# Attention tiles of 32 rows: scores from 64x32 weight tiles, value products from 32x64 weight tiles, one turn per head pair

## The chip, the cores and the metric

The kernel is one program on one core of a Trainium2 chip. The metric is the device time of that program in microseconds (us). Its engines are named as in the profile: PE is the matrix engine (PEld its weight loads), DVE the vector engine, ACT the scalar engine, POOL the GpSimd engine, SP the queue that issues the DMAs.

## The reference

Eight batches of eight heads, 576 positions, head size 64. The first four heads look back 32 positions, the last four look back 128 positions in steps of 4. Then comes a mixing block on the 512 joined channels.

```python
mask_plain = (rel >= 0) & (rel < window)                       # window = 32
mask_dil = (rel >= 0) & (rel < window * dilation) & (rel % dilation == 0)   # dilation = 4
scores = np.where(masks, scale * np.matmul(q, k.transpose(0, 1, 3, 2)), -1e9)
attn = softmax(scores)
x = np.matmul(attn, v)          # joined over the heads: (8, 576, 512)
theta = x @ w_theta
y = einsum('ts,bsd->btd', w_tok_r, x * cos(theta)) + einsum('ts,bsd->btd', w_tok_i, x * sin(theta))
u = x + y
return u + np.maximum(u @ w_ch, 0.0)
```

All arithmetic is to float32 accuracy. The host only puts q, k and v in other orders; heads with steps of 4 are put in the order position mod 4, position div 4, so that every head looks back 32 rows.

## The kernel before, in words

**Work.** A batch b has four head pairs pr (two heads hh = 0, 1 in each). The 576 query rows of a head are cut into 18 blocks of QB = 32 rows. Block qb needs the 64 key columns from 32 before its start to its end (BW = 64). Two blocks (e = 0, 1) of both heads make one group of 128 rows, so that a pair has NJ = 9 groups j.

**Scores** (`scores`, L585). The host writes q with zeros: for each block a 128x64 weight tile, whose rows are the two heads' 64 channels, and whose columns are head 0's 32 queries (rows of head 1 zero) and head 1's (rows of head 0 zero). A product of that tile with 64 key columns (L614) gives 64 rows of scores, two for a group, 18 a pair, in two PSUM banks (groups 0 to 4, 5 to 8). DVE adds the mask and takes the row maximum (L553), ACT takes the exponential (L649), DVE the sum and its reciprocal (L652, L653), POOL multiplies (L655). The result is P, 128 rows by 9 x 64.

**Turn** (`turn`, L659). The value product needs P with keys on the partitions. DVE turns P in eight transposes of 32 rows by 288 (L673), for hh, e and o (o is the first or second 32 of the 64 keys), into pt, a tile with zeros set once by POOL, where group j and head hh have a 128x64 block: rows of e = 0 against columns of e = 0, rows of e = 1 against columns of e = 1, zeros between. For batch 0 `flip` (L691) does it on PE (L709), with copies by DVE (L684) and ACT (L687).

**Value products** (`pv`, L757). For a group and a head, 128 rows of v (the two blocks' 64 keys) by 64 channels are the weights, and pt's 128x64 block moves (L773): 18 products a pair, into one PSUM tile "o" of 576 columns. ACT copies it to x (L733), for the last two pairs in the natural order of positions.

**The rest.** theta (L842), sine and cosine, and the token mixing in split form, high and low parts of about half the bits each. From batch 2 on the token mixing is done in fourteen "steps" (L1235, `fast_step`, PSUM tiles A to D) instead of L1444; then channel mixing (L1477).

**What sets the order.** A recorder (`Order`) keeps tasks with ranks and planned costs and writes the instructions of all engines in the order in which its plan starts them. In the first part (batch 0, batch 1 up to its token mixing) ranks decide (`RANK`). From batch 1's token mixing on (`steady`, `phase`) PE's order is a written list: scores of the next batch's pairs are put before steps by `S_FAST`, value products behind steps by `PV_FAST`, so that three of a batch's four score blocks stand right behind a value product. Costs in `yield "PE", ...` and in `phase` only move the plan.

**Loads.** SP loads q (576 KB a pair), k (304 KB), v in two parts (320 and 256 KB), two pairs ahead.

Of the kernel before, what the change touches and what calls it, by code (L numbers as in the profile page):

```python
# [18 lines left out]
DM = H * D  # L19
# [4 lines left out]
VA = 5  # L24
NC = DM // 128
# [187 lines left out]
SLACK = 500  # L213
LATENCY = dict(PE=100.0, DVE=100.0, ACT=130.0, POOL=130.0, DMA=1800.0)
# [35 lines left out]
def build(ctx, tc, qT, kT, vw, wth, wtk, wch, maskb, ident, identb, outT):  # L250
# [60 lines left out]
    def load_qk(n):  # L311
        if n >= B * NP:
            return
        b, pr = divmod(n, NP)
        yield "rank", due.get(("scores", b, pr), od.rank)
        r = yield from take("qk", 2)
        if od.steady and b > FIRST and pr < 2:
            yield None, ("vbi", b - 1, pr + 1)
        q = ap.tile([128, 2 * NJ, 2 * QB], F32, tag="q", name=f"q{b}_{pr}")
        k = ap.tile([128, S + 32], F32, tag="k", name=f"k{b}_{pr}")  # L320
        yield "DMA", dma(2 * S)
        pin(nc.sync.dma_start(q, qT[b, pr]))
        yield "DMA", dma(S + 32)
        pin(nc.sync.dma_start(k, kT[b, pr]))
        qks[b, pr] = (q, k, r)
        signal(("qk", b, pr))
# [51 lines left out]
    KE = S + 32  # L378
# [11 lines left out]
    mskb = cp.tile([128, 6, BW], BF16, name="mskb")  # L390
# [5 lines left out]
    def first_loads():  # L396
# [3 lines left out]
        for pr in range(NP):  # L400
# [4 lines left out]
            q = q.rearrange("p a b -> p (a b)").rearrange("p (a b) -> p a b", b=2 * QB)  # L405
            k = first_k[:, KE * pr:KE * pr + KE]
            yield "DMA", dma(2 * S)
# [19 lines left out]
    def consts():  # L427
# [4 lines left out]
        for n in range(2):  # L432
            t = cp.tile([128, NJ, 2, 2 * QB], F32, name=f"pt{n}")
            yield "POOL", 1040
            pin(nc.gpsimd.memset(t, 0.0))
            pts.append(t)
# [99 lines left out]
    def mask_of(pr, j):  # L536
        if j == 0:
            return 1
        return {2: 2, 4: 3, 6: 4, 7: 5}.get(j, 0) if pr >= NP // 2 else 0

    pmats, probs = {}, {}

    def strips():

        for hh in range(2):
            for e in range(2):
                for o in range(2):
                    yield hh, e, o
# [9 lines left out]

    def on_pe(b, pr):
        return b == 0  # L560
# [24 lines left out]
    def scores(b, pr):  # L585
        yield None, ("qk", b, pr)
        if b == 1 and on_pe(b, pr):
            yield None, "sin0"
# [11 lines left out]
        for g0, g1 in ((0, 5), (5, NJ)):  # L600
            ps, rel = yield from bank("s", f"s{b}_{pr}_{g0}")
            ps = ps[:, :(g1 - g0) * BW].rearrange("p (a b) -> p a b", b=BW)
            held[g0] = ps, rel
            if b == 2 and not od.steady:
                yield "LATER", SLACK
            masked = on_pe(b, pr)
            if masked:
                yield "PE", 150
                mask_on_pe(ps, pr, g0, g1)
            yield "PE", (148 if od.steady else 162) * (g1 - g0)  # L610
            for n in range(g0, g1):
                for e in range(2):
                    qb = 2 * n + e
                    pe(nc.tensor.matmul(ps[64 * e:64 * e + 64, n - g0], q[:, qb],  # L614
                                        k[:, QB * qb:QB * qb + BW], start=not masked, stop=not masked or n == g1 - 1))
            if masked:
                go(row_max(b, ps, rel, P, mx, g0, g1, ("mask", b, pr, g0)))
            else:
                go(mask_scores(ps, rel, P, mx, pr, g0, g1, ("mask", b, pr, g0)))
# [7 lines left out]
        if b and on_pe(b, pr):  # L627
            for g0, (ps, rel) in held.items():
                yield None, ("mask", b, pr, g0)
                yield "EXP", 335 * ps.shape[1]  # L630
                for n in range(ps.shape[1]):
                    table(nc.scalar.activation(P[:, g0 + n], ps[:, n], AF.Exp, bias=mx[:, g0 + n:g0 + n + 1],
                                               scale=SCALE, accum_out=sm[:, g0 + n, :1]))
                give(*rel)
        else:
            for g0 in (0, 5):
                yield None, ("mask", b, pr, g0)
# [5 lines left out]
        elif not on_pe(b, pr):  # L643
# [15 lines left out]
    def turn(b, pr):  # L659
# [4 lines left out]
        yield None, ("pv",) + divmod(b * NP + pr - 2, NP)  # L664
        P, rp = probs.pop((b, pr))
        pmats[b, pr] = pts[pr % 2]
        for i, (hh, e, o) in enumerate(strips()):
            if od.steady:
                yield "TURN" if i < 7 else "DVE", 482
            elif i % 2 == 0:  # L670
                yield "DVE", 940
            k0, p0 = QB * (2 * e + o), QB * (2 * e + hh)
            pin(nc.vector.transpose(pmats[b, pr][k0:k0 + QB, :, hh, QB * e:QB * e + QB],  # L673
                                    P[p0:p0 + QB, :, QB * o:QB * o + QB]))
        give("P", rp)
        signal(("pt", b, pr))

    def flip_evac(b, ps, rel, pr, g0, g1, key):
        for e in range(2):
            es, qs = slice(BW * e, BW * e + BW), slice(QB * e, QB * e + QB)  # L680
            n = (g1 - g0) * BW
            if e == 0:
                yield "DVE", dve(n)
                pin(nc.vector.tensor_copy(pmats[b, pr][es, g0:g1, :, qs], ps[es]))  # L684
            else:
                yield "ACT", act(n)
                pin(nc.scalar.copy(pmats[b, pr][es, g0:g1, :, qs], ps[es]))  # L687
        give(*rel)
        signal(key)

    def flip(b, pr):  # L691

        yield None, ("P", b, pr)
        if pr >= 1:
            yield None, ("fl", b, pr - 1)
        if b or pr >= 2:
            yield None, ("pv",) + divmod(b * NP + pr - 2, NP)
        yield None, "pts"
        pmats[b, pr] = pts[pr % 2]
        P, rp = probs.pop((b, pr))  # L700
        gs = (0, 5), (5, NJ)
        for i, (g0, g1) in enumerate(gs):
            ps, rel = yield from bank(FL0[i] if b == 0 else "xt"[i], f"pT{b}_{pr}_{g0}")
            ps = ps[:, :(g1 - g0) * BW].rearrange("p (a h b) -> p a h b", h=2, b=QB)
            yield "PE", 70 * (g1 - g0)
            for n in range(g0, g1):
                for e in range(2):
                    es = slice(BW * e, BW * e + BW)
                    pe(nc.tensor.matmul(ps[es, n - g0].rearrange("p a b -> p (a b)"), P[es, n], idt[es, es],  # L709
                                        start=True, stop=True))  # L710
            go(flip_evac(b, ps, rel, pr, g0, g1, ("fe", b, pr, g0)))
        signal(("fl", b, pr))
        for g0, _ in gs:
            yield None, ("fe", b, pr, g0)
        if b == 0:
            give(f"xh{pr}", 0)
        else:
            give("P", rp)
# [4 lines left out]
    def x_evac(b, pr, ps, rel, key):  # L723
        dst, src = xf[b, pr], ps
        if pr >= NP // 2:
            dst = dst.rearrange("p (j c) -> p c j", c=4)
            src = src.rearrange("p (c j) -> p c j", c=4)
# [29 lines left out]
    def pv(b, pr):  # L757
# [10 lines left out]
        ps = ps_v.tile([128, 2 * DM], F32, tag="v", name=f"o{b}_{pr}")[:, :S]  # L768
        yield "PE", 1060 if od.steady else 1300
        for j in range(NJ):  # L770
            v = va[:, j] if j < VA else vb[:, j - VA]
            for hh in range(2):
                pe(nc.tensor.matmul(ps[64 * hh:64 * hh + 64, BW * j:BW * j + BW], v[:, 64 * hh:64 * hh + 64],  # L773
# [963 lines left out]
```

## Time and profile before

| | |
|---|---|
| three runs, us | 555.21, 554.04, 555.28 (median 555.21) |
| profiled execution, us | 555.45 |
| its span, first to last instruction, us | 553.7 |
| granted PE clock, mean | 0.994 |
| busy, us: PE, PEld, DVE, ACT, POOL | 528.7, 478.8, 435.5, 373.1, 329.4 |
| instructions on PE and PEld | 5296 each |
| data moved by DMA | 124.42 MB, mean 225 GB/s |

The span is the time between the first and the last instruction; 1.75 us of the profiled execution lie outside it. A float32 product appears as two records on PE and two on PEld: the 18 score products of a pair are 36 records. A matmul record is long (222 ns for 64 columns), since it holds the way through the array; what counts is the distance from one record's start to the next. In rows of instructions "128*64 128x64" means a weight tile of 128 rows by 64 columns, and an output or operand of 128x64.

### The profile page before, as it was taken

Reading aid. Unit: us, or ns where it says so; the run is one execution under the profiler, and the core shown is the slowest. Engines: PE = TensorE matmul, PEld = TensorE weight load, DVE = VectorE, ACT = ScalarE, POOL = GpSimd, SP = SyncE. Lnnn points to the kernel's source line nnn. Section 1 sums busy time; section 2 is a strip of 40 time slices with the busy share of each in tenths; the row PEclk is TensorE's granted clock in tenths of the full one; section 3 lists DMA queues with packets and bytes.
Section 4 is the critical chain, followed back from the end, with each engine's and each line's share of the span. In section 5 each row is a group of like instructions: output and inputs, shape, how many; then the busy total and the mean of one; then the engine's idle time right before and its main releaser. Section 6 shows DMA issues by size and latency. Waiting matters only on the chain.

```text
span 553.7 us, 14354 instructions
## 1 busy us (share of the span) xinstructions
PE 528.7 (95%) x5296; PEld 478.8 (86%) x5296; DVE 435.5 (79%) x1359; ACT 373.1 (67%) x1029; POOL 329.4 (59%) x347
## 2 busy tenths in 40 slices
PE   5798898999999999999999999999999999999997
PEld 4643887888899899989999899989999899989997
DVE  3878897995588797989799988989799978848322
ACT  1589977858928478768775786768776777467320
POOL 1327868899774175655468375646468365817660
PEclk9999799999999999999999999999999999999999
DMA  8985245633578938994599828993698727680722
GB/s 297 400 332 186 99 139 202 222 144 119 165 256 265 343 155 283 341 282 173 189 326 306 299 86 274 363 281 118 236 325 282 277 90 219 209 274 28 233 85 86
DMA packets 59127, 124.42 MB, mean 225 GB/s; under 512 B 5424, under 2 KB 24624, under 8 KB 58800
## 3 DMA queue, kind: packets, MB, share of 16 engines
q1 hardware_dynamic: 59056, 123.49, 65.1%
q8 instruction: 42, 0.69, 0.5%
q14 instruction: 29, 0.24, 0.1%
HBM read 99.88 MB, written 23.59 MB: 223 GB/s over the span
## 4 chain that ended last, share of the span: by engine, by line
PE 65%; DVE 10%; DMA 9%; ACT 7%; POOL 5%; issue 2%; SPq 1%; POOLq 0%; ACTq 0%; DVEq 0%
PE c L1477 15%; PE th L842 11%; PE C L1235 8%; PE A L1235 7%; PE D L1235 6%; PE o L773 5%; PE B L1235 4%; PE s L614 4%; DVE pt L673 4%; DMA va<-in_vw_dram 3%; PE y L1444 2%; PE th L824 2%; DMA xn<-xd 1%; DMA st_wtk<-in_wtk_dram 1%; DMA q<-in_qT_dram 1%
## 5 line engine op out<-in xcount | busy, mean ns | idle before, releaser
L673 DVE STREAM_TRANSPOSE pt<-P 32x288 f32<-32x288 f32 x224 | 105.1, 469 | 13.1 <-POOL P L655 8.8
L1477 PE MATMUL c<-u,late_wc 128*128 128x288 f32 x768 | 109.1, 296 | 1.2 <-DVE x L1453 1.0
L1477 PEld LDWEIGHTS c<-u,late_wc 128*128 128x128 f32 x768 | 105.5, 188 | 4.7 <-DVE x L1453 1.5
L649 ACT ACTIVATE P<-P,mx 128x64 f32<-128x64 f32 x252 | 84.4, 337 | 2.9 <-DVE mx L553 2.6
L842 PE MATMUL th<-wthh,xh 128*128 128x512 f32 x224 | 75.0, 395 | 0.2 <-DVE K L1377 0.2
L655 POOL TENSOR_TENSOR P<-P,mx 128x576 f32<-128x576 f32 x32 | 38.2, 1192 | 57.6 <-DVE mx L653 50.4
L553 DVE CUSTOM_DVE_ANT_0 P<-s,mskb 128x64 f32<-128x64 f32 x252 | 39.0, 218 | 18.0 <-PE s L614 17.7
L1251 ACT CAST u<-x 128x288 fp32r<-128x288 f32 x48 | 20.6, 430 | 45.3 <-DVE x L1261 44.8
L842 PEld LDWEIGHTS th<-wthh,xh 128*128 128x128 f32 x224 | 42.0, 188 | 9.6 <-DVE K L1377 0.4
L1253 POOL TENSOR_TENSOR u<-x,u 128x288 fp32r<-128x288 f32 x48 | 41.6, 872 | 14.4 <-ACT u L1251 14.0
L649 ACT ACTIVATION_READ_ACCUMULATOR P<-P,mx 128x1 f32 x252 | 47.3, 188 | 0.0
L842 PE MATMUL th<-wthl,xh 128*128 128x512 f32 x112 | 44.4, 396 | 0.0
L733 ACT COPY x<-o 128x576 f32<-128x576 f32 x32 | 29.4, 920 | 19.6 <-PE o L773 19.5
L489 POOL TENSOR_TENSOR zl<-g,zh 128x512 fp32r<-128x512 f32 x7 | 9.1, 1298 | 53.5 <-ACT zh L481 53.5
L614 PE MATMUL s<-k,q 128*64 128x64 f32 x1008 | 36.6, 225 | 2.7 <-DVE K L1377 2.2
L614 PEld LDWEIGHTS s<-k,q 128*64 128x64 f32 x1008 | 32.8, 139 | 7.1 <-issue 2.7
L1453 DVE SCALAR_TENSOR_TENSOR x<-c,x 128x288 f32<-128x288 f32 x64 | 28.4, 451 | 11.6 <-PE c L1477 11.4
L773 PEld LDWEIGHTS o<-pt,va 128*64 128x64 f32 x600 | 20.4, 137 | 11.7 <-DVE pt L673 3.2
L773 PE MATMUL o<-pt,va 128*64 128x64 f32 x600 | 24.8, 227 | 5.8 <-DVE pt L673 2.9
L1015 POOL TENSOR_TENSOR s<-f,x 128x256 f32<-128x256 f32 x24 | 17.8, 740 | 12.2 <-DVE f L1003 10.0
L842 PEld LDWEIGHTS th<-wthl,xh 128*128 128x128 f32 x112 | 21.0, 188 | 4.2
L1095 POOL TENSOR_TENSOR s1l<-s,s1h 128x512 fp32r<-128x512 f32 x12 | 15.4, 1288 | 14.0 <-ACT s1h L1092 14.0
(232 smaller groups left out, 1576.3 us busy)
## 6 DMA issues: line engine op xcount, KB each, us to landing
q<-in_qT_dram SPq DMA_DIRECT2D x32, 576.0 KB, 6.0
late_wt_a<-tw_t SPq DMA_DIRECT2D x24, 576.0 KB, 6.8
wt_g<-tw_b SPq DMA_DIRECT2D x22, 576.0 KB, 6.4
va<-in_vw_dram SPq DMA_DIRECT2D x30, 320.0 KB, 4.9
k<-in_kT_dram SPq DMA_DIRECT2D x28, 304.0 KB, 6.2
out_dram<-x SPq DMA_DIRECT2D x28, 288.0 KB, 2.1
vb<-in_vw_dram SPq DMA_DIRECT2D x29, 256.0 KB, 4.5
xd<-xq SPq DMA_DIRECT2D x24, 288.0 KB, 5.3
```

What stands on the lines that cost most here:

```text
L553: pin(nc.vector.tensor_tensor_reduce(out=P[:, n], in0=ps[:, n - g0], in1=mskb[:, mask_of(pr, n)], op0=ALU.add, op1=ALU.min, scale=-SCALE, ...
L614: pe(nc.tensor.matmul(ps[64 * e:64 * e + 64, n - g0], q[:, qb], k[:, QB * qb:QB * qb + BW], start=not masked, stop=not masked or n == g1 - 1))
L649: table(nc.scalar.activation(P[:, n], P[:, n], AF.Exp, bias=mx[:, n:n + 1], scale=-1.0, accum_out=sm[:, n, :1]))
L655: pin(nc.gpsimd.tensor_tensor(P, P, mx.unsqueeze(2).to_broadcast([128, NJ, BW]), op=ALU.mult))
L673: pin(nc.vector.transpose(pmats[b, pr][k0:k0 + QB, :, hh, QB * e:QB * e + QB], P[p0:p0 + QB, :, QB * o:QB * o + QB]))
L733: pin(nc.scalar.copy(dst, src))
L773: pe(nc.tensor.matmul(ps[64 * hh:64 * hh + 64, BW * j:BW * j + BW], v[:, 64 * hh:64 * hh + 64], pmats[b, pr][:, j, hh], start=True, stop=T ...
L842: pe(nc.tensor.matmul(pt, l, r, start=(n == 0), stop=(n == 3 * NC - 1)))
L1235: pe(nc.tensor.matmul(ps, l, r, start=first and n == 1, stop=last and n == 3 * len(ks), skip_group_check=more))
L1253: pin(nc.gpsimd.tensor_tensor(ul[b, d][:, ts], x[:, ts], uh[b, d][:, ts].bitcast(F32), op=ALU.subtract))
L1453: pin(nc.vector.scalar_tensor_tensor(out=x[:, ts], in0=ps, scalar=0.0, in1=x[:, ts], op0=ALU.max, op1=ALU.add))
L1477: pe(nc.tensor.matmul(ps, l[:, cs], r[:, ts], start=(n == 0), stop=(n == 3 * NC - 1)))
```

## The change

Queries are stored without zeros. A head's 576 rows are cut in two halves of 9 blocks: e is now the half, and group n has block n of both halves of both heads (qb = n + 9 e). A score product has a weight tile of 64 rows (one head's channels) by 32 queries. A pair has 36 of them instead of 18, each with 64 key columns, written to one 32-row strip of a bank. For batches from 1 on the two banks are both taken first, and the products go in turn to the first bank and the second. The host swaps the two heads in the second bank's groups, so that the eight products for one group of each bank have eight different places in the array: two halves of its rows by four quarters of its columns.

The turn is one transpose of 128 rows by 576 (each 32x32 block in place), in batch 0 too; `flip`, its copies, the zeroed pt tiles and their POOL memsets are gone. A value product has 32 rows of v (one head, one half e, keys o) by 64 channels as its weights, and 32 columns of pt move. A pair has 72 of them instead of 18; the two products o = 0, 1 of a group accumulate in the same place, so that four places of the array are used (four quarters of its rows; e and the head pick them, the head picks the half of its columns). The halves e go to two PSUM banks.

q is 288 KB a pair instead of 576, k 352 instead of 304, v the same size in another order. The plan's costs are other numbers.

```diff
-        q = ap.tile([128, 2 * NJ, 2 * QB], F32, tag="q", name=f"q{b}_{pr}")
-        k = ap.tile([128, S + 32], F32, tag="k", name=f"k{b}_{pr}")
+        q = ap.tile([128, 2 * NJ, QB], F32, tag="q", name=f"q{b}_{pr}")
+        k = ap.tile([128, KE], F32, tag="k", name=f"k{b}_{pr}")
...
-                    pe(nc.tensor.matmul(ps[64 * e:64 * e + 64, n - g0], q[:, qb],
-                                        k[:, QB * qb:QB * qb + BW], start=not masked, stop=not masked or n == g1 - 1))
+        def block(n, e):
+            qb = n + NJ * e
+            ko = QB * (qb + 1 + 2 * e + (n >= JS)) - QB
+            for r in range(2):
+                rs, to = slice(64 * r, 64 * r + 64), QB * (2 * e + (r if n < JS else 1 - r))
+                ps = held[0 if n < JS else JS][0]
+                pe(nc.tensor.matmul(ps[to:to + QB, n % JS], q[rs, qb], k[rs, ko:ko + BW],
+                                    start=b > 0, stop=b > 0 or n in (JS - 1, NJ - 1)))
...
+            yield "PE", SC_NS
+            for i in range(JS):
+                for g0, g1 in groups:
+                    if g0 + i < g1:
+                        for e in range(2):
+                            block(g0 + i, e)
...
-            pin(nc.vector.transpose(pmats[b, pr][k0:k0 + QB, :, hh, QB * e:QB * e + QB],
-                                    P[p0:p0 + QB, :, QB * o:QB * o + QB]))
+        pin(nc.vector.transpose(pmats[b, pr], P.rearrange("p n (o s) -> p (n o) s", s=QB)))
...
-            for hh in range(2):
-                pe(nc.tensor.matmul(ps[64 * hh:64 * hh + 64, BW * j:BW * j + BW], v[:, 64 * hh:64 * hh + 64],
-                                    pmats[b, pr][:, j, hh], start=True, stop=True))
+            for o in range(2):
+                for e in range(2):
+                    for hh in range(2):
+                        rs = slice(QB * (2 * e + hh), QB * (2 * e + hh) + QB)
+                        pe(nc.tensor.matmul(ps[64 * hh:64 * hh + 64, e, QB * j:QB * j + QB], v[rs, 64 * o:64 * o + 64],
+                                            pmats[b, pr][rs, 2 * j + o], start=(o == 0), stop=(o == 1)))
...
-        go(flip(0, p), RANK["flip"][p])
+        go(turn(0, p), RANK["flip"][p])
```

PE's list at one place of the steady part, before: between step products into D and C stand the value products of the third pair (o_3) and the scores of the next batch's pair 1 (s_1_0 and s_1_5 are its two banks). "x10" is ten equal products in a row.

```order
L1235 MATMUL D_1_4941<-late_wt_b,s1l_4799 128x288
L773 MATMUL o_3_4972<-pt_118,va_3_4756 64x64 x10
L773 MATMUL o_3_4972<-pt_118,vb_3_4836 64x64 x8
L614 MATMUL s_1_0_4997<-k_1_4759,q_1_4758 64x64 x10
L614 MATMUL s_1_5_5018<-k_1_4759,q_1_4758 64x64 x8
L1235 MATMUL C_0_4865<-late_wt_a,i2h_4889 128x288 x2
```

The same place of the changed kernel:

```order
L1184 MATMUL D_1_5232<-late_wt_b,s1l_5030 128x288
L724 MATMUL o_3_5262<-pt_117,va_3_4980 64x32 x40
L724 MATMUL o_3_5262<-pt_117,vb_3_5112 64x32 x32
L595 MATMUL s_1_0_5341<-k_1_4983,q_1_4982 32x64 x4
L595 MATMUL s_1_5_5342<-k_1_4983,q_1_4982 32x64 x4
L595 MATMUL s_1_0_5341<-k_1_4983,q_1_4982 32x64 x4
L595 MATMUL s_1_5_5342<-k_1_4983,q_1_4982 32x64 x4
L595 MATMUL s_1_0_5341<-k_1_4983,q_1_4982 32x64 x4
L595 MATMUL s_1_5_5342<-k_1_4983,q_1_4982 32x64 x4
```

The blocks keep their places among the steps; 18 and 18 products have become 72 and 36, and the scores alternate between the banks.

DVE's list in the last batch before, where pair 2's and pair 3's turns (L673) stand among additions of step results (L1261, L1273):

```order
L673 STREAM_TRANSPOSE pt_116<-P_2_6357 32x9x32
L1261 TENSOR_TENSOR x_0_5508<-B_0_6462,x_0_5508 128x288
L673 STREAM_TRANSPOSE pt_116<-P_2_6357 32x9x32
L1261 TENSOR_TENSOR x_1_5639<-B_1_6480,x_1_5639 128x288
L652 TENSOR_REDUCE mx_3_6434<-sums_97 128x9
L653 RECIPROCAL mx_3_6434<-mx_3_6434 128x9
L673 STREAM_TRANSPOSE pt_116<-P_2_6357 32x9x32 x6
L1273 TENSOR_TENSOR x_2_5713<-A_0_6381,x_2_5713 128x288
L673 STREAM_TRANSPOSE pt_118<-P_3_6433 32x9x32
```

The same place now (the turn is L662, xq is the turn of x for the batch after):

```order
L1210 TENSOR_TENSOR x_0_7031<-B_0_8316,x_0_7031 128x288
L662 STREAM_TRANSPOSE pt_116<-P_2_8125 128x576
L1210 TENSOR_TENSOR x_1_7234<-B_1_8330,x_1_7234 128x288
L645 TENSOR_REDUCE mx_3_8274<-sums_97 128x9
L646 RECIPROCAL mx_3_8274<-mx_3_8274 128x9
L846 STREAM_TRANSPOSE xq_8318<-x_1_8395 128x18x32
L1222 TENSOR_TENSOR x_2_7356<-A_0_8165,x_2_7356 128x288
L662 STREAM_TRANSPOSE pt_117<-P_3_8273 128x576
```

Each pair's eight transposes have become one, and the additions stand closer together.

More of the change, by code (lines that the diff above doesn't have):

```diff
@@ L432, in consts @@
         for n in range(2):
[L433 to L436, printed above, removed]
+            pts.append(cp.tile([128, 2 * NJ, QB], F32, name=f"pt{n}"))
         signal("pts")
@@ L536, in mask_of @@
     def mask_of(pr, j):
-        if j == 0:
-            return 1
-        return {2: 2, 4: 3, 6: 4, 7: 5}.get(j, 0) if pr >= NP // 2 else 0
+        if pr < NP // 2:
+            return int(j == 0)
+        return {0: 2, 4: 3, 5: 4}.get(j, 0)
     pmats, probs = {}, {}
-    def strips():
-        for hh in range(2):
-            for e in range(2):
-                for o in range(2):
-                    yield hh, e, o
     def mask_scores(ps, rel, P, mx, pr, g0, g1, key):
@@ L603, in scores @@
             held[g0] = ps, rel
+            if b == 0:
+                yield "PE", 150
+                mask_on_pe(ps, pr, g0, g1)
+                yield "PE", 125 * (g1 - g0)
+                for n in range(g0, g1):
+                    for e in range(2):
+                        block(n, e)
+                go(row_max(b, ps, rel, P, mx, g0, g1, ("mask", b, pr, g0)))
+        if b:
             if b == 2 and not od.steady:
                 yield "LATER", SLACK
[L606 to L614, printed above, removed]
-                                        k[:, QB * qb:QB * qb + BW], start=not masked, stop=not masked or n == g1 - 1))
-            if masked:
-                go(row_max(b, ps, rel, P, mx, g0, g1, ("mask", b, pr, g0)))
-            else:
+            yield "PE", SC_NS
+            for i in range(JS):
+                for g0, g1 in groups:
+                    if g0 + i < g1:
+                        for e in range(2):
+                            block(g0 + i, e)
+            for g0, g1 in groups:
+                ps, rel = held[g0]
                 go(mask_scores(ps, rel, P, mx, pr, g0, g1, ("mask", b, pr, g0)))
@@ L626, in scores @@
             go(load_qk(b * NP + pr + 2), RANK["load"][0])
[L627 to L637, printed above, removed]
+        for g0 in (0, JS):
+            yield None, ("mask", b, pr, g0)
         if b == 0:
@@ L663, in turn @@
         yield None, ("P", b, pr)
-        yield None, ("pv",) + divmod(b * NP + pr - 2, NP)
+        if b or pr >= 2:
+            yield None, ("pv",) + divmod(b * NP + pr - 2, NP)
         P, rp = probs.pop((b, pr))
         pmats[b, pr] = pts[pr % 2]
[L667 to L673, printed above, removed]
-                                    P[p0:p0 + QB, :, QB * o:QB * o + QB]))
@@ L675, in turn @@
[L675 to L715, printed above, removed]
+        yield "DVE", 790
@@ L716, in flip @@
+        pin(nc.vector.transpose(pmats[b, pr], P.rearrange("p n (o s) -> p (n o) s", s=QB)))
+        if b:
+            give("P", rp)
+        else:
             give(f"xh{pr}", 0)
-        else:
-            give("P", rp)
         signal(("pt", b, pr))
@@ L1570, in steady @@
             prev = key
-            if key[0] == "sc" and not on_pe(*key[1:]):
+            if key[0] == "sc":
                 go(turn(*key[1:]), t)
```

83 lines of the change are left out of this document (44 added, 39 removed).

## The prediction

> **What bounds the kernel now.** I read the busy times by stretch first, then the waits of PE, then the chain that ended last, then PE's timeline at one place of it.
>
> The stretches (length, busy time and count of PE, PEld, DVE, ACT, POOL, then clock, DMA share, GB/s) and the longest waits of PE on DVE (total, times, longest):
>
> ```profile
> 0.00:166.00 166.00, 145.57 (x1615) 119.02 (x1615) 127.87 (x389) 117.35 (x308) 112.76 (x113) 0.98 0.61 213
> 166.00:500.00 334.00, 333.05 (x3319) 310.95 (x3320) 284.73 (x919) 238.99 (x687) 189.26 (x204) 1.00 0.74 249
> 500.00:553.70 53.70, 50.03 (x364) 48.78 (x363) 22.93 (x55) 16.75 (x36) 27.36 (x32) 1.00 0.32 111
> ...
> PE o L773 <- DVE pt L673: 2.9, 2, 1.7
> PE s L614 <- DVE K L1377: 2.2, 1, 2.2
> PE y L1444 <- DVE mx L553: 1.1, 1, 1.1
> PE c L1477 <- DVE x L1453: 1.0, 2, 0.8
> PE xn L933 <- DVE K L924: 1.0, 1, 1.0
> ```
>
> From 166 to 500 us PE misses 0.95 of 334 us, at full clock: there the time is PE's list, and what DVE, ACT or DMA gain is worth nothing. Before 166 us PE idles 20 us, of which these five waits on DVE are 8.2. The chain in the steady part is PE alone (start, length, what):
>
> ```profile
> 328.81 1.20 PE s L614 x36
> 330.01 2.58 PE A L1235 x18
> 332.59 1.20 PE o L773 x36
> 333.79 1.05 PE s L614 x36
> 334.84 2.59 PE B L1235 x18
> ```
>
> A score block costs 1.20 us between products of full weight tiles, and 1.05 right behind a value block, whose tiles have the same shape; a change of shape is worth 0.15. The chain at the start is made of loads:
>
> ```profile
> 3.07 5.78 DMA q<-in_qT_dram
> 8.87 10.37 DMA va<-in_vw_dram
> 19.32 6.10 DMA st_wtk<-in_wtk_dram
> ```
>
> **How fast small tiles go.** All hangs on what a round of tiles costs. PE's timeline, groups by shape (mean ns of one is the second number behind the bar), the shortest, middle and longest value record, and a window that ends at 344.346:
>
> ```profile
> 22.71 1.26 PE L709 MATMUL pT<-ids,P 64*64 64x64 f32 x36 [0.48 <-POOL P L655]
> 38.84 1.09 PE L933 MATMUL xn<-ids,x 128*128 128x128 f32 x8
> 345.44 1.22 PE L614 MATMUL s<-k,q 128*64 128x64 f32 x36
> 346.59 0.54 PE L1235 MATMUL C<-wt_g,s3h 128*128 128x288 f32 x2
> ...
> L614 PE MATMUL s<-k,q 128*64 128x64 f32 x1008 | 36.6, 225 | 2.7 <-DVE K L1377 2.2 <-issue 0.5
> L933 PE MATMUL xn<-ids,x 128*128 128x128 f32 x9 | 1.6, 288 | 0.4 <-DVE Kg L924 0.4
> L824 PEld LDWEIGHTS th<-st_wth,x 128*128 128x128 f32 x28 | 4.6, 188 | 5.1 <-issue 2.6 <-DMA st_wtk<-in_wtk_dram 0.9 <-DVE st_wtk L465 0.9
> L709 PEld LDWEIGHTS pT<-ids,P 64*64 64x64 f32 x88 | 2.9, 134 | 2.3 <-issue 1.6 <-POOL P L655 0.6
> L824 PEld LDWEIGHTS th<-st_wth,x 128*64 128x64 f32 x8 | 0.8, 134 | 2.5 <-issue 2.4
> ...
> L773 PE MATMUL o<-pt,va x600: 222/222/270, 25.4 to 476.7; 128*64 128x64 f32 x150
> 344.34 0.28 PE L773 MATMUL o<-pt,va 128*64 128x64 f32 x2
> ```
>
> Eight records of 128 columns on the whole array take 1.09 us; less one length of 0.29 that is seven distances, 114 ns each, 57 for 64 columns. The 36 score records of 64 columns take 1.22; less one length of 0.22 that is 1.00 over 35 distances, 29 ns each. So two tiles run side by side, and a round of two takes 58 ns. The window shows it: the first two records of a block, the long ones of 0.27, start before it ends and together span 0.28. Starting a record thus costs some 6 ns, the page's rounding included.
>
> A record also needs its weights. The load of 128 columns is 188 ns long, that of 64 columns 134, with 128 rows and with 64 rows: 64 columns cost 54 ns, rows nothing. Streaming 64 columns and loading 64 columns both fill the present round; the trace can't say which of them sets it. The change parts them.
>
> **Scores.** 72 records, eight at a time: 9 rounds. Streaming is still 64 columns, the load 32 (27 ns): the round stays 58, so 0.53 us; filling eight places costs 8 x 6 = 0.05. Against 1.05 that is -0.47 a block. The bound by starts alone is 72 x 6 = 0.43 us, no tighter.
>
> **Value products.** 144 records, four at a time: 36 rounds. Streaming is 32 columns (27 ns), but the load is still 64 columns, 54 ns, and now twice as many loads stand behind each other in each place. Bounds of a round: 31 ns if loads don't count (27 + 4), 58 if the load sets it (54 + 4), 85 if load and stream of a place follow each other (54 + 27 + 4). The last has no row on its side: today's round of 58 holds 54 of both, so they overlap. I take 58: 36 x 58 = 2.10 against 1.05, +1.05 a block; the ends are +0.07 and +2.0.
>
> The Trainium skill, "TensorE: Matmul & The Clock Gate", section "LDWEIGHTS (loading the stationary operand)", says the same against this change: a load takes columns / 1.2 ns, whatever the rows, 53 ns here; by that alone a block would be 36 x 53 = 1.92 us and the forecast 5 us lower. No run here shows a tile of 32 rows.
>
> **Change of shape.** Scores behind a value block now change shape: +0.15 (from 0 to 0.24).
>
> **The sum on PE.** The steady part proper begins behind these rows of the chain:
>
> ```profile
> 166.82 1.41 PE o L773 x36
> 168.23 1.05 PE s L614 x36
> ```
>
> By then the value blocks of batches 1 and 2 are done (8) and the scores of batches 1 and 2 and of two pairs of batch 3 (10). Left are 20 and 18; three of four scores stand behind a value block, in the last round one of two, 13 in all: 20 x 1.05 - 18 x 0.47 + 13 x 0.15 = +14.5 us, nothing beside it to hide it. Before, 8 value blocks, 10 score blocks, 3 pairs of them: 8.4 - 4.7 + 0.45 = +4.2; this too lies in PE's list.
>
> **DVE.** The turns and their new form's nearest row:
>
> ```profile
> L673 DVE STREAM_TRANSPOSE pt<-P 32x288 f32<-32x288 f32 x224 | 105.1, 469 | 13.1 <-POOL P L655 8.8
> L897 DVE STREAM_TRANSPOSE xq<-x 128x576 f32<-128x576 f32 x24 | 17.7, 762 | 1.0 <-ACT x L733 0.9
> ```
>
> 28 turns go from 8 x 0.469 = 3.75 us to 0.76, 84 us of DVE in all. PE waits for DVE only before 166 us, 8.2 us in the rows above; the DVE that works there loses some 8 x 3 = 24 of 128 us. I take 5 of the 8.2 (0 to 8.2).
>
> **Loads.** q and k of batch 0 stand at the head of SP's queue, ahead of v and the mixing weights that the chain waits for:
>
> ```profile
> 20.00:40.00 20.00, 18.04 (x239) 10.02 (x240) 15.67 (x32) 14.19 (x24) 4.42 (x3) 1.00 1.00 380
> ...
> q<-in_qT_dram SPq DMA_DIRECT2D x4, 576.0 KB, 6.4
> first_k<-in_kT_dram SPq DMA_DIRECT2D x4, 304.0 KB, 6.7
> ```
>
> 4 x (288 - 48) KB = 0.98 MB at 380 GB/s is 2.6 us, all taken (0 to 5, with the flip's copies gone). Later loads lie under PE, at a DMA share of 0.74.
>
> **Edits at nothing.** Batch 0 swaps flips for four turns on DVE, and its value blocks add 4 x 1.05 where its scores and flips drop more; the loads cover both, else some 2 us either way. The copy of "o" (L733) has another pattern and the same size; PE covers it. Scores wait for two free banks instead of one, with steps queued behind them on PE; the banks were last read several us earlier, and a step's length (2.6 us) is the price of each miss.
>
> **Total.** 555.45 (the profiled execution, 0.24 above the median) + 14.5 + 4.2 - 5 - 2.6 = 566.55; against the median 566.3. Own range: 556 (a round of 54, all waits and 5 us of loads won: 4.4 + 3.2 + 2.4 less) to 576 (none won, changes of shape at 0.24: 7.6 + 1.4 more).
>
> **Rivals.**
> 1. *Loads don't set the round; faster.* If a place of 32 rows gets its 64 columns in half the time or less, a value block is 36 x 31 = 1.12 us: 20 x 0.07 - 8.5 + 2.0 = -5.1, early 0.6 - 4.7 + 0.45 = -3.7, with -7.6 as above: 538.8. For it speaks that 54 ns is known only for 64 and 128 rows, and a number of the code: its plan takes 1060 ns for a value block before, which the chain shows as 1.20, and 1100 for the new one, which would be this case if it is as near. Against it stands that 64 and 128 rows agree, 134 and 134. It decides at a round of 47 ns: there 28 x (36 x 47 - 1050 ns) eats what scores, DVE and loads give. The Trainium skill, "TensorE: Matmul & The Clock Gate", section "Measured speedup vs the span model", has tiles side by side cost one matmul and some 4 ns for each further tile, and names no load; by it this rival would be the case. In this trace the 6 ns agree, for two tiles.
> 2. *Places that share columns don't run side by side; slower still.* In the trace, tiles side by side have different columns; the change also puts row halves and quarters over the same ones. Scores would go four at a time, 18 rounds, and win nothing: 28 x 0.47 = 13 us more, 579.5; value blocks of 4.2 us in the worst case would add 60. The Trainium skill, "TensorEngine Tiling (Array Packing)", section "Gotcha 1: PSUM Pressure", has a rule near it: row tiles cannot use one PSUM bank at once. The flips speak against it in that form: two tiles of 64 rows write two strips of one bank, and 36 records take 1.26 us, no more than two places of the same rows do.
> 3. *The round is 58, but the start gives more.* This is my low end, 556, within 0.3% of the median.
>
> **Chances.** Forecast 0.56, rival 1 0.36, rival 2 0.05, equal (rival 3; within 0.3%, 1.7 us, about what can be told here) 0.03. Faster 0.36, same 0.03, slower 0.61. Both signs are open, so the range for 8 in 10 takes in both, rival 1 down to 535 (more waits and loads won, 3 to 4 us): 535 to 577.
>
> **What would show it.** Right: value blocks (L724) of about 2.1 us with 144 records, PEld's record for 32x64 tiles as long as today's for 64 columns, about 134 ns, scores (L595) of 0.6 us plus 0.15 for the change of shape, PE without idle time from about 165 us, a batch some 2.8 us longer than now, L662 at 0.76 us. Wrong: value blocks near 1.1 us (rival 1), scores of 1 us or more (rival 2), or new waits on PE in the steady part.

## The result, and the profile after

The changed kernel takes 654.4 us (651.8 to 654.9) against 555.3 (554.0 to 556.2): a ratio of 1.178, interval 1.174 to 1.182. The profiled execution took 654.5 us with a span of 652.7, against 555.5 and 553.7. The forecast was 566.3, with 577 as the upper end.

The stretches of the changed kernel (the columns are those shown of before: length, busy time and count of PE, PEld, DVE, ACT, POOL, then clock, DMA share, GB/s). Three rows are steady batches, cut where the batch's first score block starts:

```profile
166.00:239.50 73.50, 68.21 (x1136) 63.26 (x1136) 37.47 (x127) 37.41 (x113) 31.58 (x38) 0.93 0.64 203
239.50:317.70 78.20, 69.67 (x1214) 65.07 (x1214) 42.45 (x158) 47.47 (x138) 39.97 (x45) 0.93 0.59 188
317.70:394.50 76.80, 69.08 (x1215) 64.49 (x1216) 41.47 (x152) 45.23 (x133) 35.47 (x39) 0.93 0.59 190
394.50:467.90 73.40, 68.37 (x1209) 63.91 (x1208) 41.33 (x152) 45.03 (x133) 35.42 (x39) 0.95 0.63 199
```

A batch of before, cut in the same way:

```profile
267.30:328.70 61.40, 61.40 (x633) 57.48 (x632) 54.33 (x182) 45.23 (x134) 36.72 (x40) 1.00 0.75 254
```

It was 61.4 us long with PE busy all through it, at full clock. Now a batch takes 73 to 78; PE is idle for 5 to 9 us of it, and the clock is below 1. The longest waits of PE, and its longest ones for DVE (total, times, longest):

```profile
PE s L595 <- issue: 25.7, 12, 3.9
PE o L724 <- issue: 17.2, 9, 3.9
PE y L1393 <- ACT wtkh L480: 5.2, 1, 5.2
...
PE s L595 <- DVE K L1326: 2.3, 1, 2.3
PE th L791 <- DVE g L871: 1.9, 1, 1.9
PE xn L882 <- DVE Kg L873: 1.0, 1, 1.0
PE th L791 <- DVE K L1326: 0.9, 1, 0.9
PE s L557 <- DVE P L566: 0.9, 1, 0.9
```

"issue" means that no engine, no transfer and no semaphore of the profile is waited for. These waits stand in the middle of a block, whose products all have their data. The chain that ended last, in one part of a steady batch (start, length, what):

```profile
335.76 3.39 PE A L1184 x24
339.14 2.23 PE o L724 x144
341.38 0.24 PE s L595 x7
341.61 3.94 issue
345.56 1.19 PE s L595 x62
346.75 6.04 PE C L1184 x30
```

PE's timeline at the same place, and at the next score block that ran through:

```profile
336.18 0.43 PE L1184 MATMUL A<-late_wt_a,s2h 128*128 128x288 f32 x2
336.45 0.29 PE L1184 MATMUL A<-late_wt_a,s2l 128*128 128x288 f32 x1
336.59 0.42 PE L1184 MATMUL A<-late_wt_a,s2h 128*128 128x288 f32 x2
...
347.56 0.68 PE L1184 MATMUL C<-wt_g,s3h 128*128 128x288 f32 x2
348.04 0.44 PE L1184 MATMUL C<-wt_g,s3l 128*128 128x288 f32 x1
348.28 0.68 PE L1184 MATMUL C<-wt_g,s3h 128*128 128x288 f32 x2
...
359.62 0.97 PE L595 MATMUL s<-k,q 64*32 64x64 f32 x72
360.52 0.53 PE L1184 MATMUL C<-late_wt_a,i2h 128*128 128x288 f32 x2
```

Three records of 288 columns take 0.41 us ahead of the pause (336.18 to 336.59) and 0.72 behind it (347.56 to 348.28). So a pause is paid twice: once while PE stands, and again while it runs slower afterwards. The undisturbed blocks are near the forecast: values 2.23 us to the next product (the chain's row at 339.14), scores 0.90 (359.62 to 360.52).

What is short is PE's own instructions. They come by transfers on a queue that the profile page lists in its third section (packets, MB, share); first before, then after:

```profile
q8 instruction: 42, 0.69, 0.5%
```

```profile
q8 instruction: 76, 1.25, 0.8%
```

Each transfer is 16,384 bytes. PE and PEld together have 10,592 records before and 19,504 after, 252 and 257 a transfer: a block of 256 instructions of 64 bytes. The table follows the trace's transfers around the pause shown above (us). It counts every instruction that PE and PEld have started, the 141 semaphore and drain instructions among their records too. The limit is the count at which PE stood, or would have stood if the block had not come: 449, and 256 more for each block before this one.

```
block  starts  landed   done at start   limit   next record after a pause
38     318.70  320.12    9763            9921   no pause
39     324.13  325.07   10177           10177   326.57
40     328.89  329.86   10247           10433   no pause
41     335.24  336.58   10549           10689   no pause
42     343.20  344.17   10945           10945   345.56
```

In block 39's row PE has done 10177 instructions, the limit, when the transfer starts, and its next record comes 1.5 us after the block has landed. PE stops exactly at a limit when the block that carries it on has not come. In this kernel and the ten below, from 240 us on, 83 of the 89 pauses of PE over 0.6 us stand at such a count; a pause ends 1.1 to 1.6 us after the block has landed. A transfer itself takes 0.9 to 1.9 us, 1.0 in the middle, before and after alike; two of them start at least 3.4 us apart in the changed kernel, so that the supply is at most some 256 / 3.4 = 75 instructions a us. A value block asks for 288 in 2.2 us and a score block for 144 in 0.9. Before, both together asked for 144 in 2.3 us, and the step products between them ask for some 14 a us (18 records and their loads in 2.58 us).

The Trainium skill, "Runtime: NRT & Kernel Launch", section "Instruction fetch mechanics", describes the blocks of 256 instructions, and the trace agrees (252 and 257 records a transfer). It goes on that fetching stays hidden, since an engine needs some 20 cycles for each instruction. Here the trace differs: the 72 score records and their 72 loads start within 0.76 us, 5 ns for each instruction, and PE runs dry.

Where the 99 us are, by the distances between PE's records (a distance over 0.6 us counts as a pause; us before, after, difference; "early" ends where the first batch with steps begins, 205.9 and 239.5):

```
                          early                  from there on
value blocks          14.4  33.0  +18.6        23.0  45.3  +22.3
score blocks          20.2  16.9   -3.3        20.9  16.9   -4.0
flips                  5.1   0     -5.1         0     0      0
all other products   142.2 143.8   +1.6       300.2 314.7  +14.5
pauses at a limit      2.7  15.3  +12.6         0    32.0  +32.0
other pauses          18.2  27.5   +9.3         0     0.8   +0.8
sum                              +33.7                    +65.6
```

### The profile page after: what moved, and what is told of

The parts are those of the page before. It is cut to its first block, busy times and chain, and to the rows that moved or that the text cites. A ratio compares the mean times of both kernels' runs of the same rounds, so it can differ in the third digit from the quotient of the medians.

```text
span 652.7 us, 23049 instructions
## 1 busy us (share of the span) xinstructions
PE 582.8 (89%) x9752; PEld 528.4 (81%) x9752; DVE 349.2 (53%) x1159; ACT 371.0 (57%) x1021; POOL 324.7 (50%) x345
## 4 chain that ended last, share of the span: by engine, by line
PE 78%; issue 8%; ACT 5%; DVE 4%; DMA 3%; SPq 1%; POOL 1%; DVEq 0%; POOLq 0%; ACTq 0%
PE c L1426 12%; PE o L724 12%; PE th L791 10%; PE C L1184 9%; PE y L1393 9%; PE D L1184 6%; PE A L1184 6%; PE s L595 5%; PE B L1184 4%; PE th L773 2%; DMA xd<-xq 1%; DMA xn<-xd 1%; PE th L796 1%; ACT P L642 1%; PE th L795 1%
## 5 line engine op out<-in xcount | busy, mean ns | idle before, releaser
L595 PE MATMUL s<-k,q 64*32 64x64 f32 x2016 | 32.0, 243 | 27.0 <-issue 24.4
L595 PEld LDWEIGHTS s<-k,q 64*32 64x32 f32 x2016 | 24.8, 114 | 32.6 <-issue 28.9
L1202 POOL TENSOR_TENSOR u<-x,u 128x288 fp32r<-128x288 f32 x48 | 38.2, 804 | 18.2 <-ACT u L1200 18.1
L724 PEld LDWEIGHTS o<-pt,va 32*64 32x64 f32 x2400 | 39.8, 138 | 9.1 <-issue 3.9
L724 PE MATMUL o<-pt,va 32*64 32x32 f32 x2400 | 43.1, 223 | 3.4 <-issue 2.8
L724 PE MATMUL o<-pt,vb 32*64 32x32 f32 x1856 | 35.6, 223 | 8.9 <-issue 8.9
L724 PEld LDWEIGHTS o<-pt,vb 32*64 32x64 f32 x1856 | 32.5, 140 | 8.5 <-issue 8.5
L1184 PE MATMUL C<-wt_g,s3h 128*128 128x288 f32 x96 | 25.7, 363 | 3.1 <-issue 3.1
L1210 DVE TENSOR_TENSOR x<-C,x 128x288 f32<-128x288 f32 x24 | 10.9, 456 | 27.1 <-PE C L1184 27.1
```

The source lines that it names most:

```text
L595: pe(nc.tensor.matmul(ps[to:to + QB, n % JS], q[rs, qb], k[rs, ko:ko + BW], start=b > 0, stop=b > 0 or n in (JS - 1, NJ - 1)))
L724: pe(nc.tensor.matmul(ps[64 * hh:64 * hh + 64, e, QB * j:QB * j + QB], v[rs, 64 * o:64 * o + 64], pmats[b, pr][rs, 2 * j + o], start=(o == ...
L1184: pe(nc.tensor.matmul(ps, l, r, start=first and n == 1, stop=last and n == 3 * len(ks), skip_group_check=more))
L1202: pin(nc.gpsimd.tensor_tensor(ul[b, d][:, ts], x[:, ts], uh[b, d][:, ts].bitcast(F32), op=ALU.subtract))
```

## The experiments

The theory: PE's instructions are supplied at some 75 a us at most, with about 300 or fewer in hand when a transfer starts; small tiles use them up in bursts, PE stands, and then runs at half clock. Rivals: the small tiles disturb each other (shared columns, banks, accumulation); a longer value block does it by itself; the half clock belongs to small tiles and not to the pauses. "Pauses" below are those of 0.45 us and more at a limit, behind 165 us: 36.4 us in 15 in the changed kernel (the expectations speak of 38, from a first reading), none before.

**e1_scores**: before, with the new score blocks alone (the smaller q and k, and the planner's cost of a score block, change with them).

```diff
-        for e in range(2):
-            pe(nc.tensor.matmul(ps[64 * e:64 * e + 64, n - g0], q[:, qb], k[:, QB * qb:QB * qb + BW], ...
+        for r in range(2):
+            rs, to = slice(64 * r, 64 * r + 64), QB * (2 * e + (r if n < JS else 1 - r))
+            pe(nc.tensor.matmul(ps[to:to + QB, n % JS], q[rs, qb], k[rs, ko:ko + BW], ...
```

> The kernel before with the new score tiles alone (64x32, eight at once over two banks; q and k in their new, smaller layout); value blocks, flips and turns as before. The theory (small tiles are paid for by instructions: PE's instructions come in blocks of 256 and the supply keeps up with some 75 a us, with about 300 in hand): a score block has 144 PE and PEld instructions instead of 72 but takes 0.75 to 0.80 us instead of 1.05, a value block before it only 72, together 216, fewer than are in hand. So no stall on issue over 0.5 us behind 165 us, clock at 1.00, and the time falls by 18 blocks x 0.27 = 4.9 us in the steady part and up to 2.6 us at the start: about 548 (545 to 552). Rival one, that tiles which share columns or two banks conflict in themselves: stalls of 1 us and more in the middle of the score blocks as in the changed kernel (there 26 us in steps of 2 to 4), about 575. Rival two, that the gaps are waits for data or DMA: none here either, but then also none in the other kernels of this call.

Measured: 568.4 us, ratio 1.024 (1.021 to 1.028). By its total this is far from my 548. Steady batches took 60.6 to 61.2 us, with one pause, of 0.66 us, where I had expected none over 0.5. So the steady part came out nearly as the theory says and the total did not: the first batch with steps begins at 220.4 us instead of 205.9. That stretch has waits which are none of the theory's, since the planner had put the work of all engines in another order:

```profile
PE th L849 <- DVE g L929: 5.9, 1, 5.9
PE y L1451 <- ACT late_wt_b L482: 5.4, 1, 5.4
PE xn L940 <- DVE K L931: 4.7, 1, 4.7
```

The run also shows half clock far from any small tile (the nearest are score blocks at 175 and 220 us). Products of 512 columns ahead of and behind the first of these waits:

```profile
199.66 0.39 PE L849 MATMUL th<-wthh,xh 128*128 128x512 f32 x1
199.89 0.39 PE L849 MATMUL th<-wthl,xh 128*128 128x512 f32 x1
...
207.98 0.76 PE L849 MATMUL th<-wthh,xh 128*128 128x512 f32 x1 [5.87 <-DVE g L929]
208.54 0.63 PE L849 MATMUL th<-wthl,xh 128*128 128x512 f32 x1
208.97 1.05 PE L849 MATMUL th<-wthh,xh 128*128 128x512 f32 x2
```

0.23 us apart before it, 0.43 behind it.

**e2_values**: the changed kernel with the old score blocks (the lines with - above for those with +; q and k are as large as before again, and the planner's costs of a score block go with it).

> The changed kernel with the old zero-padded 128x64 score tiles (and q and k as large as before); values from 32x64 tiles and the one turn stay. The theory: a value block still takes 2.1 us and 288 instructions, the score block 72 in 1.05 us: 360 in 3.2 us, near what is in hand, so most stalls go: under 12 us of stalls on issue behind 165 us instead of 38, few stretches at half clock. Time 555.5 + 28 x 1.05 - 5 + 8 of stalls + 5 of clock: about 590 (580 to 605). Rival, that the value tiles themselves stall (sharing columns, accumulating in place): the stalls inside value blocks stay as they are, some 17 to 25 us and the half clock behind them, about 625 to 650.

Measured: 644.8 us, ratio 1.159 (1.152 to 1.165); pauses of 26.8 us in 12. By time this is the rival's window, and my size was wrong: 360 instructions in 3.4 us (2.23 and 1.20) are far over the supply, too. But the place speaks against the rival. Waits of this kernel, where L592 are score blocks of the old shape:

```profile
PE o L719 <- issue: 15.2, 11, 3.1
PE s L592 <- issue: 13.8, 5, 4.0
```

Half of the waiting is in tiles that never waited before; it comes where the instructions end, not where tiles are small.

**e3_apart**: the changed kernel, the same products, other places.

```diff
-S_FAST = {2: 0, 3: 1, 4: 6, 5: 10}
-PV_FAST = {0: 0, 1: 3, 2: 5, 3: 9}
+S_FAST = {2: 0, 3: 2, 4: 8, 5: 12}
+PV_FAST = {0: 0, 1: 4, 2: 6, 3: 9}
```

> The changed kernel with every PE instruction kept and only the places of value and score blocks among the steps moved (score blocks before steps 0, 2, 8, 12 instead of 0, 1, 6, 10; value blocks behind steps 0, 4, 6, 9 instead of 0, 3, 5, 9), so that no score block stands right behind a value block. The theory: 288 instructions in 2.1 us, then 18 to 48 in the step products, then 144: what is in hand lasts, and the stalls on issue behind 165 us fall from 38 us to under 10, the half clock with them; 13 changes of shape more cost 2 us. Time about 654 - 30 - 25 + 2: 600 (585 to 615). Rival one, that the small tiles stall by themselves: same instructions, same stalls, 650 and more. Rival two, that the half clock is the answer to small tiles and not to the stalls: stalls go but the clock stays at 0.92, about 620 to 630.

Measured: 631.5 us, ratio 1.136 (1.129 to 1.142); pauses of 18.5 us in 12. The direction is the theory's: nothing but the places changed, and half of the pauses and 23 us went. The size is not, since two value blocks now stand 5.6 us apart (their starts), 576 instructions in 8 us, and the longest pause, 3.2 us, is in the second.

**e5_half**: the changed kernel with half of the value weights' columns (half of the sums is left out).

```diff
-    pe(nc.tensor.matmul(ps[64 * hh:64 * hh + 64, e, ...], v[rs, 64 * o:64 * o + 64], ..., start=(o == 0), stop=(o == 1)))
+    pe(nc.tensor.matmul(ps[64 * hh + QB * o:64 * hh + QB * o + QB, e, ...], v[rs, 64 * o:64 * o + QB], ..., start=True, stop=True))
```

> The changed kernel with value weights of 32 columns instead of 64: each product loads half its columns, the two row halves write into different rows of the output without being added (half of the value sums is left out); the number of instructions is the same. If the weight load sets the round of 32x64 tiles, the round falls from 58 to about 31 ns and an undisturbed value block from 2.08 to 1.1 to 1.2 us. If something else sets it (four places in turn, accumulation), it stays near 2. For the theory of the instruction supply: PE's list is then 28 us shorter, but 432 instructions come in 2 us instead of 3, so the stalls grow by about as much as the blocks lose: stalls on issue behind 165 us of 45 to 60 instead of 38, and the time falls by 10 at most (645 to 655). By a rival without a supply limit it falls by the 28 us, to 626.

Measured in one run: 644.6 us, 0.4 below my range. PE's timeline at one pair of blocks:

```profile
331.93 0.85 PE L724 MATMUL o<-pt,va 32*32 32x32 f32 x78
...
332.63 0.72 PE L724 MATMUL o<-pt,vb 32*32 32x32 f32 x62
333.28 0.31 PE L595 MATMUL s<-k,q 64*32 64x64 f32 x7
337.94 1.19 PE L595 MATMUL s<-k,q 64*32 64x64 f32 x65 [4.35 <-issue]
```

A value block takes 1.35 us (331.93 to 333.28), so the load of 64 columns did set the round. 28 blocks are 25 us shorter, pauses grew from 36.4 to 47.6 us in 20, and the time fell by 10, about as expected. Doing less on PE is paid back as waiting.

**e4_wide**: the changed kernel with 64 moving columns for each value product (wrong values in the further columns).

```diff
-    pmats[b, pr][rs, 2 * j + o], ...
+    pmats[b, pr][rs, min(2 * j + o, 2 * NJ - 2):][:, :2], ...
```

> The changed kernel with value products that stream 64 columns instead of 32 (weights and number of instructions kept; the further columns are wrong values and x is not the reference's). If the load of 64 columns sets the round, a block stays at 2.08 us between its first and last record and the time at 654 (645 to 660). If load and stream follow each other in a place, or if the round is bound by streaming at four places, the block grows to 3 us or more and the time by 25 us or more, less what longer blocks save in stalls.

Measured in one run: 646.4 us, a block of 2.26 us against 2.23. Twice the columns cost nothing beside the load, and the two runs settle what sets the round.

**e6_split**: before, each value product in two halves of 32 moving columns.

```diff
+    for h in range(2):
         for hh in range(2):
-            pe(nc.tensor.matmul(ps[64 * hh:64 * hh + 64, BW * j:BW * j + BW], v[:, 64 * hh:64 * hh + 64], pmats[b, pr][:, j, hh], ...
+            c = BW * j + QB * h
+            pe(nc.tensor.matmul(ps[64 * hh:64 * hh + 64, c:c + QB], v[:, 64 * hh:64 * hh + 64], pmats[b, pr][:, j, hh, QB * h:QB * h + QB], ...
```

> The kernel before, nothing of the change, but each of its value products is split into two halves of 32 columns (with the 128x64 weights loaded for each): 36 rounds of two places as in the changed kernel 36 rounds of four, but 144 PE and PEld instructions a block instead of 288. If the weight load of 64 columns sets the round, a block goes from 1.05 to 2.1 us as it did with 32x64 tiles; if the stream sets it, to about 1.1. For the theory of the instruction supply: 144 + 72 instructions behind each other are no burst that empties what is in hand, so no stall on issue behind 165 us, clock 1.00, and the time is 555.5 + 28 x 1.05 = 585, less what the early part hides (578 to 587). By the rival that longer value blocks bring the stalls and the low clock by themselves, 640 and more.

Measured: 589.6 us, ratio 1.059 (1.055 to 1.063), 2.6 us above my range and far below the rival's 640. A steady batch, and a value block of it with the score block behind:

```profile
349.10:414.70 65.60, 65.60 (x779) 61.70 (x778) 54.42 (x180) 45.35 (x134) 36.42 (x40) 1.00 0.71 237
```

```profile
366.77 1.36 PE L774 MATMUL o<-pt,va 128*64 128x32 f32 x40
367.96 1.10 PE L774 MATMUL o<-pt,vb 128*64 128x32 f32 x32
368.89 1.25 PE L614 MATMUL s<-k,q 128*64 128x64 f32 x36
```

Value blocks of 2.12 us, as long as the changed kernel's, but with half as many instructions: no pause at a limit behind 165 us, full clock, a batch of 61.4 + 4 x 1.05. The rival of the longer block falls.

**e7_parts**: the changed kernel, value blocks of the steady batches in two parts behind steps of their own.

```diff
-S_FAST = {2: 0, 3: 1, 4: 6, 5: 10}
-PV_FAST = {0: 0, 1: 3, 2: 5, 3: 9}
+S_FAST = {2: 0, 3: 4, 4: 8, 5: 13}
+PV_FAST = {0: (0, 1), 1: (4, 5), 2: (6, 8), 3: (9, 10)}
...
-        for j in range(NJ):
+        for j in range(0 if part != 1 else VA, NJ if part != 0 else VA):
```

> The changed kernel, every product kept, with the value blocks of the steady batches cut in two (40 and 32 products, 160 and 128 instructions) and the parts and the score blocks each put behind a step of their own, at least 12 step products (1.6 us) apart. The theory: by stretches of some 5 us the list then asks for at most about 66 instructions a us, which the supply gives: stalls on issue from 240 us on under 5 us instead of 32 in the changed kernel and 16 in the one with blocks moved as a whole, and no half clock there; a steady batch of about 66 us instead of 77. The time about 605 (592 to 615). Rival, small tiles stall by themselves: as many stalls, 650. Rival, the half clock comes from small tiles: stalls go, but the batches still take some 70 us, 622.

Measured: 628.2 us, ratio 1.128 (1.123 to 1.133). By time, and by batches of 69.1 to 70.7 us, this is near the second rival, and the clock has to decide. From 240 us on the pauses are 9.5 us instead of 32, none over 2.2. A steady batch:

```profile
449.50:518.60 69.10, 67.18 (x1215) 61.47 (x1217) 43.28 (x152) 46.01 (x134) 36.03 (x41) 1.00 0.66 211
```

With the small tiles all there the clock is 1.00, in this batch and in one more; the other two are at 0.98, each with one stretch of 3.4 us at half clock, behind pauses of 1.3 and 1.6 us. So the half clock belongs to the pauses, not to the tiles. The early part stayed as it was: the first batch with steps begins at 237.9 us, against 239.5 in the changed kernel and 205.9 before. My 66 us a batch left out the changes of shape. By its distances, this batch is 61.5 of before + 4.2 for values - 1.1 for scores + 2.1 for changes of shape + 2.4 of pauses = 69.1.

**e8_plan**: e1_scores with the planner's costs of before, which was to keep PE's list as it was.

```diff
-            yield "PE", 800
+            yield "PE", (148 if od.steady else 162) * NJ
```

> The new score tiles alone once more, but with the planner's costs left as before, so that PE's list is the list of the kernel before with each score block in its place. If the 13 us that the score tiles alone lost lie in the early part, in waits for DVE and ACT that came with another order of the work (steady batches there were 61.0 us against 61.4), they go: 555.5 - 5 - 2 = 548 (545 to 552). If they come from the small score tiles themselves, 560 to 568 again.

Measured: 561.6 us, ratio 1.009 (1.006 to 1.012). I had forecast 548, and by time this is the other reading, that small score tiles lose by themselves; e10_late below tests it again. Steady batches take 60.7 to 60.8 us, and the first begins at 216.0, 10 us late. The edit did not do what it was for. In the early part PE's list, too, is still another (39 records of the channel mixing stand ahead of the theta products of 121.7 us, 33 ahead of the same ones at 113.1 before), and so is the order of DVE, ACT and POOL. PE waits 4.6 us for K of DVE and 4.7 for weights of POOL. The costs alone moved the total by 7 us.

**e9_quarters**: before, each score and value product from batch 1 on cut in four, with all its 128 rows.

```diff
+    for h in range(0, BW, m):
         for hh in range(2):
-            pe(nc.tensor.matmul(ps[64 * hh:64 * hh + 64, ...], v[:, 64 * hh:64 * hh + 64], pmats[b, pr][:, j, hh], ...
+            for r in range(64 * hh, 64 * hh + 64, m):
+                pe(nc.tensor.matmul(ps[r:r + m, ...], v[:, r:r + m], pmats[b, pr][:, j, hh, h:h + m], ...
```

> The kernel before with its old layouts, flips and turns, and from batch 1 on each score and value product cut in four: 32 of its weight columns by 32 of its moving columns, with all 128 rows as before. No row tiling, no accumulation and the same sums, but a block has 288 PE and PEld instructions instead of 72. If a record starts every 10 ns, as the new score blocks show, a block takes some 1.4 us instead of 1.05, so a pair of value and score block asks for 576 instructions in 2.9 us. The theory of the instruction supply: stalls on issue in the middle of these blocks as in the changed kernel or longer, 13 us or more a steady batch, each of 2 us and more followed by half clock; a batch of some 80 us instead of 61.4, the time 655 (635 to 680). Rival, the stalls belong to tiles of 32 or 64 rows, that is to places that share columns: none here, 555.5 + 24 x 0.7 = 572 (565 to 580).

Measured: 684.2 us, ratio 1.227 (1.222 to 1.232). Its longest waits, its timeline at one pair of blocks, and one of its batches:

```profile
PE s L617 <- issue: 52.7, 21, 4.9
PE o L780 <- issue: 20.4, 8, 4.7
```

```profile
340.22 0.86 PE L780 MATMUL o<-pt,va 128*32 128x32 f32 x78
...
340.93 0.71 PE L780 MATMUL o<-pt,vb 128*32 128x32 f32 x62
341.50 0.59 PE L617 MATMUL s<-k,q 128*32 128x32 f32 x45
346.69 1.60 PE L617 MATMUL s<-k,q 128*32 128x32 f32 x99 [4.60 <-issue]
```

```profile
317.60:397.40 79.80, 68.89 (x1642) 64.54 (x1641) 54.38 (x188) 45.94 (x135) 36.76 (x40) 0.94 0.60 199
```

Nothing of the change is in this kernel: no row tiles, no shared columns, the old data. It has more instructions in the same work (its tiles are also only 32 columns wide, but those of e10_late below are so too and run without a pause), and it has the changed kernel's pauses, 73.3 us in 25, and its half clock. This decides between the theory and the rival of the tiles. The size was above my 680, with 11 to 16 us of pauses in each of the four steady batches and 9.5 in the last one (62.6 from 240 us on), and a block of 1.3 us where I had said 1.4.

**e10_late**: before, with the new score blocks from batch 3 on alone.

```diff
+NEW = 3
...
+        if b >= NEW:
...
+                            pe(nc.tensor.matmul(held[g0][0][to:to + QB, i], q[rs, qb], k[rs, ko:ko + BW],
+                                                start=True, stop=True))
```

> The kernel before with the new score tiles, and the smaller q and k, from batch 3 on alone (16 blocks); the batches before that, the order of every engine's early work and the planner's costs are those of the kernel before. Both kernels with the new score tiles everywhere gained 0.9 us a steady batch and lost 10 and 14 us in the early part. If the loss was the early part's alone, this keeps the gain: 555.5 - 4 x 0.9 = 552 (550.5 to 553.5), ratio 0.994. If small score tiles bring a loss of their own in some other place, 556 or more.

Measured: 552.3 us, as forecast; ratio 0.993 (0.991 to 0.995), a little faster than before. One batch:

```profile
267.40:328.10 60.70, 60.70 (x784) 56.48 (x786) 52.53 (x180) 44.95 (x134) 35.94 (x40) 1.00 0.72 237
```

The gain of the small score tiles is real where their 144 instructions meet a value block of 72, and where nothing else is put in another order. So the losses of e1_scores and e8_plan lie in their early part; what in its order made DVE and POOL late was not settled.

## Why the prediction was wrong

- **What bounds.** That "there the time is PE's list" was read rightly of before. The step that failed is to carry it over: the sum prices a new list by its records and takes for granted that PE gets any list as fast as it can run it. The term that is missing is the supply of instructions. It cost 44.6 us of pauses at a limit (12.6 early and 32.0 later, by the table) and, behind the later ones, the 14.5 us that the other products took longer: 34 us of their time from 239.5 us on lie in stretches at half clock, where three records take 0.72 us instead of 0.41, and none did before. The profile page of before already showed both sides, 42 transfers on q8 and 5296 records each of PE and PEld; the change all but doubles the records, and the prediction counted them only to price them.
- **Value blocks.** The round of 58 ns set by the load of 64 columns was right, and so was the record of some 134 ns:

```profile
L724 PEld LDWEIGHTS o<-pt,va 32*64 32x64 f32 x2400 | 39.8, 138 | 9.1 <-issue 3.9 <-ACT st_wth L461 2.9 <-ACT P L642 1.8
L662 DVE STREAM_TRANSPOSE pt<-P 128x576 f32<-128x576 f32 x32 | 24.5, 767 | 0.0
```

  e4_wide and e5_half confirm it from both sides. The term of 20 x 1.05 = 21.0 us measured 22.3. Rival 1 falls by it.
- **Score blocks.** Eight tiles side by side over shared columns do run, so rival 2 falls, but a block takes 0.90 us with its change of shape and not 0.73. The 72 records start 10.6 ns apart, where I had 8 a round of 58, or 7.3. Whether that is a price of starting a record, above the 6 ns of the bound that I put aside, or a longer round of eight, is not shown; in e9_quarters, with four places, records start 8.9 ns apart. The term of -18 x 0.47 = -8.5 measured -4.0; with the changes of shape, the whole of 14.5 us measured 18.3.
- **Early part.** +4.2 - 5 - 2.6 was forecast and +33.7 came. Blocks and flips gave +10.2 of it, since the twelve value blocks there cost 18.6 more, 1.55 each: many run at half clock, where their loads are 222 ns long instead of 133 (row below). Pauses at a limit gave 12.6, and other waits 9.3 where 5 were to be won; the longest of these, 5.2 us, is for weights from ACT (wtkh, in the waits above). The loads left the chain, and pauses took their place: before, the chain of the first 26 us holds three loads of 22.3 us in all; now it holds one, of 3.8 us, and five waits on issue between 13 and 39 us, 9.4 us in all. DVE became free as forecast, from 435.5 to 349.2 us busy, but PE's waits for it did not go: the five longest were 8.2 us in all and are 7.0. The loads of value weights in batch 0 (shortest, middle and longest, ns):

```profile
L724 PEld LDWEIGHTS o<-pt,first_v x288: 128/222/227, 15.9 to 30.1; 32*64 32x64 f32 x144
```

- **L662** at 0.767 us was right (row above), and none of PE's waits is for it.
- **What would show it wrong** named "new waits on PE in the steady part" and gave them no price. They came, and for a reason that is in none of its rivals.

## What to carry to other kernels

When a change cuts products into smaller tiles, count instructions as well as time: matmuls and weight loads in every burst, and per us over some 5 us of the engine's list. Here a burst of 216 in 2.1 us passed between long products (e10_late; in e1_scores with one pause of 0.66 us), one of 360 in 3.4 us did not (e2_values), and some 75 a us is the most that lasts. Spread such blocks between long products. A pause of PE over 2 us costs its length and, by an estimate, some 1.7 us more: half of the 3.4 us at half clock that mostly follow it.

## What the runs showed that was not expected

- Instructions for PE come in blocks of 256. When a block's transfer starts, 300 are left or fewer in all twelve kernels (the table above has 186 and less), and from landing to the next record it is 1.1 to 1.6 us where PE stood. What makes a transfer start late (it is not its own 1.0 us) stays open; no run varied it.
- Half clock comes in stretches of about 3.4 us or a multiple (3.4, 6.8 and 23.9 us in the changed kernel). Of PE's pauses beyond 50 us in all twelve kernels that began at full clock, 13 of 87 between 0.8 and 2 us were followed by one (it started in the pause or within 3.4 us of its end), 19 of 24 between 2 and 2.5, and 59 of 62 above. The Trainium skill, "TensorE: Matmul & The Clock Gate", section "Part 1: The HAM clock gate", has a free-running window of 3413 ns, and the lengths agree; but the limit of some 3.4 us of idle time that its section "HAM oscillation" gives is too wide here.
